# A turn through DRAM replaced by copies between partitions, and a last stage laid between late products

## The chip, the cores and the metric

The kernel runs on one core of a Trainium2 chip. The metric is the device time of one execution in microseconds. A core has a matrix engine (TensorE, PE in the profile, with its weight loads as PEld), a vector engine (VectorE, DVE), a scalar engine (ScalarE, ACT), GpSimd (POOL), and a sync engine (SP) that here only issues DMAs. ACT and POOL issue DMAs too. All DMAs run on the core's 16 DMA engines.

## The reference

The input is a sequence of 2048 rows of 512 channels, `x = A_u`. Two branches read it, and a gate per row mixes them:

```python
g = _sigmoid((x * gate_w).sum(-1, keepdims=True))
a = _A_ref(...)   # K[d,l] = sum_n Re(C exp(dt A l) dt B); y = irfft(rfft(u) * rfft(K)) + u * Dskip
b = _B_ref(...)   # gelu(x @ w1 + b1) @ w2 + b2, with an inner width of 1792
return g * a + (1 - g) * b
```

So `a` is a long convolution of every channel with a kernel K made from 128 complex exponentials, and `b` is a dense layer pair. All is float32.

## The kernel before

The program has two parts. `front` computes the gates, the dense branch `b` (already times 1 - g, written to `out`), the taps K and the first stage of the transforms of signal and taps. Every operation of it is a task with a due time; a planner (`Plan`) orders the tasks of each engine once, while the program is built, and the upper-case constants at the head of the file (`T_MLP`, `T_KG`, `D_KP` and so on) are the due times and offsets. The first stages' results go to DRAM: `tu_d` (signal) and `tk_d` (taps), 32 rows of 256 KB each. The last 18 products of the dense branch's second layer (each three matmuls, since a float32 factor is split into a high and a low part) are not planned; `front` hands them over as the list `late`.

`conv` is written out by hand, and each engine runs its instructions in the order of the program text. It works in 16 passes `s`, two transform rows n = 2s and 2s + 1 each:

- `signal(s)` and `taps(s)`: the second stage of the transforms on PE (tiles `p2u`, `p2k`, line 1157); ACT evicts `p2k`.
- `product(s)`: six DVE operations, the complex product.
- `inverse(s)`: the first stage back, on PE, into `pa` (line 1196).
- `turn(s)`: ACT copies `pa` to one of six buffers `sa`, and the data changes its layout: what lay on 128 partitions as (part, row) must lie, for the last stage, with transform rows on the partitions. Before, SP stores `sa` to DRAM (`t_d`, named `t4_d` in the code, line 1204), in groups of 8 rows; when a group is whole, POOL (ACT for the last row of all) fetches it as blocks of 8 or 4 rows onto every fourth partition of `t3` and `den` (line 1216). Some fetches wait in a list `held` until pass 9.
- `dense(k)`: fetches two tiles of the dense branch's result from `out` into `mos[k]`, in rooms that have come free (six by SP in passes 7 to 12, two by ACT behind the passes).

The late products run on PE by `rest(n)`, which takes n from the list, into four accumulators `acc` (lines 1241 to 1243): three before the last inverse, fifteen behind it. Then DVE adds each accumulator, times its gate, to its tile in `mos` (line 1293). The last stage has 8 blocks `m` (line 1301): each makes two result tiles `pb` by 8 matmuls as the profile counts them, and each of these reads a row block on all 128 partitions of `t3` or `den`, so every block needs all 32 turned rows. A tile is evicted by DVE with gate and dense part in one step (line 1313), or, for the six tiles in `ASIDE`, by ACT and then POOL. Blocks 0 to 6 go out by SP, 512 KB each (line 1317); the two tiles of block 7 by SP and ACT, 256 KB each (line 1315).

Rooms: `attic` (11 rows of 2 KB per partition), `loft` (8) and `den` (8) outlive the front. `places` deals them to the signal's rows `us[n]`: den's 8 first, then attic and loft, then 5 again from attic. 27 rows are fetched by `front` (`early`, line 479), the other 5 in the passes. The taps' rows `t2s` have eight buffers of their own (tag `tk`), and rows 16 to 23 use rooms of `t3`.

Of the kernel before, what the change touches and what calls it, by code (L numbers as in the profile page):

```python
# [9 lines left out]
F32 = mybir.dt.float32  # L10
# [3 lines left out]
ALU = mybir.AluOpType  # L14
# [3 lines left out]
P = 128  # L18
# [16 lines left out]
T_MLP = 408.145  # L35
K_0 = 32.114
T_KG = 351.806
U_0 = 29
U_GAP = 18
LAG = 14.812  # L40
TABLE = 27.405
D_KA = -32.407
D_KP = -80.929
D_S1 = 7.912
D_EV = -40.921
D_H = -80.673
# [3 lines left out]
D_SP = -0.52  # L50
MEM = (6, 2, 3)
N_LD, N_HL, N_ST = MEM
D_XS = -157.526
D_G = 1.227
N_WARM = 13
T_EARLY, T_LOFT, T_DEN = 353.026, 381.686, 484.328
Y_K, Y_U = 44.535, 26.725
W_MLP = (-0.0644, -0.031, 0.0179)
W_KG = (-0.0372, -0.0319, -0.0262)
W_U = (-0.0347, -0.139, -0.0186)  # L60
D_MAG = -0.783
D_ROT = 0.578
D_CON = 0.705
D_PHA = 0.305
D_PRE = -3.087
D_XL = 34
D_COE = -3.192
D_OUT = -3.305
D_LAST = -1.557
N_REST = 3  # L70
D_KA0 = 0
D_DT = 5
D_PRM = -277.043
D_D0 = -1024.07
D_WAVE0 = -343.734
D_COE0 = -66.219
D_SP1 = -461.8
D_G0 = 2
D_GW = 598.738
D_XS0 = 98.527  # L80
# [3 lines left out]
D_X0, D_B2, D_B2C, D_DM = -1313.069, -235.635, -950.754, -4.033  # L84
# [4 lines left out]
HERE, THERE = (7, 6, 0, 1, 2, 3), (4, 5)  # L89
N_DEN = 8  # L90
N_ROOM = N_ATTIC + N_LOFT
N_US = N_DEN + N_ROOM

GROUP = 8
# [19 lines left out]

def seat(n, c, kind):

    return 4 * (16 * kind + 2 * (n % 8) + c) + n // 8
# [11 lines left out]
def constants():  # L129
# [39 lines left out]
    g2 = np.zeros((32, 64, 32, 2))  # L169
    for n, k in enumerate(ko):  # L170
        er, ei = om(4 * np.outer(q - 31.5, k + 32 * k1) + (q - 31.5)[:, None])
        f2[n, 0], f2[n, 1] = er, -ei
        a = 2.0 * np.pi * (k + 32 * k1 + 0.25) / L
        g2[n, :, :, 0] = np.cos(np.outer(a, m))
        g2[n, :, :, 1] = np.sin(np.outer(a, m))
        g2[n, :, 0, 1] = 1 - 2 * (k1 % 2)
# [131 lines left out]
def gated_mix(  # L308
# [24 lines left out]
    t4_d = dr.tile([4, 2, GROUP, 2, 32, D], F32, name="t4_d")  # L333
# [11 lines left out]
    def places(attic, loft, den):  # L345

        rooms = [attic[:, k] for k in range(N_ATTIC)] + [loft[:, k * D : k * D + D] for k in range(N_LOFT)]
        return [den[:, k] for k in range(N_DEN)] + rooms + rooms[: 32 - N_US]

    def front(pool, psum, keep, attic, loft, den):  # L350
# [113 lines left out]
        def early():  # L464

            us = places(attic, loft, den)
            keys = [("ux", 0)] + [("st", k) for k in range(N_ST)]
            keys = [*keys, *(("ld", k) for k in range(N_LD)), "gwb"]
            yield 1e6
            for n in range(N_US):  # L470
                m = n - N_DEN
                if m < 0:
                    due, key = T_DEN + n, [("xc", n // 4)]
                elif m < N_ATTIC:
                    due, key = T_EARLY + 2.5 * m, [keys[m]]
                else:
                    due, key = T_LOFT + m, ["xt", "xv"] if m < N_ATTIC + 4 else ["tt"]
                move(
                    256, lambda n=n: nc.sync.dma_start(us[n], tu_d[k0_order()[n]]), due,
                    [("u_d", k) for k in range(64)], key,  # L480
                )
            yield None
# [636 lines left out]
    def conv(pool, ps, late, attic, loft, den):  # L1119
# [4 lines left out]
        us = places(attic, loft, den)  # L1124
# [73 lines left out]
        def turn(s):  # L1198

            for n in (2 * s, 2 * s + 1):  # L1200
                sa = sas[n % 6]
                nc.scalar.copy(sa, pas.pop(n))
                g, k = divmod(n, GROUP)
                nc.sync.dma_start(t4_d[g, :, k].rearrange("e c q d -> (c q) e d"), sa)
# [4 lines left out]
                for h in (0, 4, 8, 16, 24) if g == 3 else (0, 8, 16, 24):  # L1209
                    if h == 24 and g < 2:  # L1210
                        held.append((t3[g:P:4, 16:24], rows[:, 24:32]))
                        continue
                    on = nc.gpsimd if n < 31 else nc.scalar
                    e = h + (4 if g == 3 and h < 8 else 8)
                    to = t3[g:P:4, h - 8 : e - 8] if h > 7 else den[g:P:4, h:e]
                    on.dma_start(to, rows[:, h:e])

        accs, mos = {}, {}
        held = []

        def dense(k, on):

            q = HERE.index(k) if k in HERE else 6 + THERE.index(k)
            r = 5 + 2 * q if q < 7 else 0
# [5 lines left out]
            on.dma_start(mos[k], out[2 * k : 2 * k + 2].rearrange("s p d -> p s d"))  # L1230
# [27 lines left out]
        for s in range(16):  # L1258

            for n in range(2 * s + N_TK + (2 if s else 0), 2 * s + N_TK + 4):  # L1260
                if n < 24:
                    fetch(n if n < 16 else n + 8)
            if s == 0:
                for n in range(16, 24):
                    fetch(n)
# [11 lines left out]
            if s == 9:  # L1277
                for to, rows in held:
                    nc.gpsimd.dma_start(to, rows)
# [4 lines left out]
            if 7 <= s < 13:  # L1284
                dense(HERE[s - 7], nc.sync)
        for k in THERE:
            dense(k, nc.scalar)
        rest(18)

        for s in range(4):  # L1290
            m, i = 7 - s // 2, s % 2
            z, g = mos[m][:, i], gate[:, 1, 2 * m + i : 2 * m + i + 1]
            nc.vector.scalar_tensor_tensor(z, accs[s], g, z, ALU.mult, ALU.add)

        for m in range(8):
            tag = ("pu0", "pu1", "pu2", "pu3", "pa0", "pa1", "pk0", "pk1")
            pbs = [ps.tile([P, D], F32, tag=tag[(2 * m + i) % 8], name=f"pb{m}{i}", bufs=1) for i in range(2)]
            for i in range(2):
                for b in range(2):
                    j = 4 * m + 2 * i + b  # L1300
                    nc.tensor.matmul(  # L1301
                        pbs[i][64 * b : 64 * b + 64], g1t[:, min(j, 1)], t3[:, j - 8] if j > 7 else den[:, j],
# [13 lines left out]
            if m < 7:  # L1316
                nc.sync.dma_start(out[2 * m : 2 * m + 2].rearrange("s p d -> p s d"), mos[m])

# [4 lines left out]
    den = keep.tile([P, N_DEN, D], F32, name="den")  # L1323
# [76 lines left out]
```

## Time and profile before

| | us |
|---|---|
| timed runs: median of 3 (lowest, highest) | 520.37 (519.99, 521.77) |
| the profiled execution | 517.95 |
| its span, first to last instruction | 515.7 |
| PE busy | 501.5 |
| granted PE clock, mean | 0.995 |

The page gives the busy time of each engine, the span in 40 slices, the DMA queues, the chain of work that ended last (followed back from the last instruction to what released it), the costliest groups of instructions, and the DMA issues with their size and median time to landing. The other views used are busy times by windows, the chain in order of time, the instructions in order of time for one engine, and the instructions of one line or tile. A busy PE is not PE at its peak, since ends of matmuls are modelled; distances from start to start are safer. DMA moved 107.87 MB at a mean of 209 GB/s, 37.24 MB of it from 404 us to the end.

```
## 2 busy tenths in 40 slices
PE   7899999999999999999999999999999999999995
DVE  5999999999999996999999699979951188877543
ACT  5698846899685769995776997747733655555311
DMA  8965995522395331565753265967486998999978
```

### The profile page before, as it was taken

The numbers are of one execution on the slowest core, as the hardware profiler recorded it, in microseconds if no ns is written. First come the engines' busy times: TensorE is split into PE (matmuls) and PEld (weight loads), VectorE is DVE, ScalarE is ACT, GpSimd is POOL, SyncE is SP. The second block draws the span as 40 slices with busy tenths as digits, with TensorE's granted clock in tenths as the row PEclk, the third lists the DMA queues.
The fourth block names the chain that finished last, engine by engine and source line by source line (L and its number), as shares of the span: only waits on it lengthen the run. The fifth ranks groups of instructions, "written<-read, shape, count | busy, mean of one in ns | idle before, by whom it ended". The sixth has DMA issues, their size and how long they took to land.

```text
span 515.7 us, 12196 instructions
## 1 busy us (share of the span) xinstructions
PE 501.5 (97%) x4810; PEld 385.1 (75%) x4810; DVE 427.5 (83%) x792; ACT 349.6 (68%) x625; POOL 42.6 (8%) x82
## 2 busy tenths in 40 slices
PE   7899999999999999999999999999999999999995
PEld 6797898899888989898888977888989742222551
DVE  5999999999999996999999699979951188877543
ACT  5698846899685769995776997747733655555311
POOL 3000000000000000001001020101010100020113
PEclk9899999999999999999999999999999999999999
DMA  8965995522395331565753265967486998999978
GB/s 293 338 229 176 319 310 172 184 85 101 109 219 163 104 124 48 177 217 145 142 186 63 84 143 135 194 205 207 132 231 159 267 391 291 372 319 401 345 280 306
DMA packets 80008, 107.87 MB, mean 209 GB/s; under 512 B 39404, under 2 KB 40560, under 8 KB 79408
## 3 DMA queue, kind: packets, MB, share of 16 engines
q1 hardware_dynamic: 73904, 85.10, 50.9%
q0 software_dynamic: 5120, 18.59, 13.5%
q10 hardware_dynamic: 928, 3.41, 1.8%
q8 instruction: 38, 0.62, 0.5%
q14 instruction: 18, 0.15, 0.1%
HBM read 61.46 MB, written 45.62 MB: 208 GB/s over the span
## 4 chain that ended last, share of the span: by engine, by line
PE 79%; ACT 7%; DVE 7%; DMA 4%; issue 1%; SPq 1%; DVEq 0%; ACTq 0%
PE pk L724 10%; PE ph L946 8%; PE acc L994 8%; PE ph L948 8%; PE ph L947 8%; PE acc L996 7%; PE acc L995 7%; PE p2u L1157 6%; PE p2k L1157 5%; PE pa L1196 3%; PE pb L1301 3%; PE ph L436 3%; DMA tk<-tk_d 1%; DMA tu_d<-attic 1%; DMA sk<-in_w_dram 1%
## 5 line engine op out<-in xcount | busy, mean ns | idle before, releaser
L946 PE MATMUL ph<-xh,wh 128*128 128x256 f32 x448 | 128.1, 286 | 3.2 <-DVE hl L976 2.9
L948 PE MATMUL ph<-xh,wl 128*128 128x256 f32 x448 | 127.6, 285 | 1.4 <-DVE wl L826 1.4
L947 PE MATMUL ph<-xlo,wh 128*128 128x256 f32 x448 | 127.0, 284 | 0.0
L946 PEld LDWEIGHTS ph<-xh,wh 128*128 128x128 f32 x448 | 85.5, 191 | 10.7 <-issue 7.0
L948 PEld LDWEIGHTS ph<-xh,wl 128*128 128x128 f32 x448 | 85.6, 191 | 2.3 <-DVE wl L826 2.3
L947 PEld LDWEIGHTS ph<-xlo,wh 128*128 128x128 f32 x448 | 85.5, 191 | 2.0
L994 PE MATMUL acc<-wh,hh 128*128 128x512 f32 x206 | 83.1, 404 | 0.0
L996 PE MATMUL acc<-wh,hl 128*128 128x512 f32 x206 | 81.0, 393 | 0.9 <-DVE hl L976 0.8
L995 PE MATMUL acc<-wl,hh 128*128 128x512 f32 x206 | 81.1, 394 | 0.0
L963 ACT ACTIVATE ph<-ph,b1t 128x256 f32<-128x256 f32 x112 | 50.5, 451 | 39.2 <-PE ph L948 37.4
L724 PE MATMUL pk<-y,den 128*32 128x64 f32 x2048 | 61.4, 290 | 0.0
L724 PEld LDWEIGHTS pk<-y,den 128*32 128x32 f32 x2048 | 57.2, 136 | 3.5 <-issue 1.8
L976 DVE TENSOR_TENSOR hl<-ph,hh 128x512 fp32r<-128x512 f32 (+1 forms) x62 | 38.1, 616 | 19.2 <-ACT hh L966 19.1
L994 PEld LDWEIGHTS acc<-wh,hh 128*128 128x128 f32 x206 | 39.0, 189 | 16.2 <-issue 8.6
L687 DVE TENSOR_TENSOR y<-y,ea 128x64 f32<-128x64 f32 (+4 forms) x80 | 45.2, 564 | 4.1 <-ACT y L677 3.3
L996 PEld LDWEIGHTS acc<-wh,hl 128*128 128x128 f32 x206 | 38.8, 189 | 10.5 <-DVE hl L976 1.8
L995 PEld LDWEIGHTS acc<-wl,hh 128*128 128x128 f32 x206 | 38.8, 189 | 6.5
L966 ACT CAST hh<-ph 128x512 fp32r<-128x512 f32 (+1 forms) x62 | 33.0, 532 | 13.6 <-PE acc L995 12.0
L530 DVE TENSOR_TENSOR loft<-den,zz 128x256 f32<-128x256 f32 (+2 forms) x48 | 37.2, 775 | 0.6
L531 DVE TENSOR_TENSOR loft<-den,zz 128x256 f32<-128x256 f32 (+2 forms) x48 | 37.1, 773 | 0.0
L699 DVE TENSOR_TENSOR y<-y,loft 128x2048 f32<-128x2048 f32 x16 | 36.5, 2283 | 0.0
L1165 ACT COPY k<-p2k 128x512 f32<-128x512 f32 x32 | 18.7, 585 | 25.1 <-issue 13.1
(194 smaller groups left out, 873.8 us busy)
## 6 DMA issues: line engine op xcount, KB each, us to landing
tu_d<-attic SPq DMA_DIRECT2D x64, 128.0 KB, 3.6
tk_d<-sk SPq DMA_DIRECT2D x32, 256.0 KB, 4.9
t_d<-sa SPq DMA_DIRECT2D x32, 256.0 KB, 5.2
tk<-tk_d SPq DMA_DIRECT2D x24, 256.0 KB, 5.1
t<-t_d POOLq DMA_DIRECT2D x9, 512.0 KB, 7.3
attic<-in_xt_dram SPq DMA_DIRECT2D x16, 256.0 KB, 4.3
attic<-in_xs_dram SPq DMA_DIRECT2D x16, 256.0 KB, 4.6
xh_d<-xh SPq DMA_DIRECT2D x8, 512.0 KB, 3.6
```

Of the source, the lines that this page charges most:

```text
L530: vec(2 * m, lambda: vv.tensor_mul(t, a, br), due, [ka, *kb], [kt])
L687: nc.vector.tensor_mul(both(n, 64 - 3 * n, n), both(0, 64 - n, n), an)
L724: nc.tensor.matmul(pks[q][32 * j : 32 * j + 32, :, gg], x[:, r, :, ch], y[:, r, :, ch], start=(r == 0), stop=(r == 1), skip_group_check=True,)
L946: nc.tensor.matmul(p, h, xh[xk][:, d], start=(d == 0), stop=False)
L947: nc.tensor.matmul(p, h, xlo[xk][:, d], start=False, stop=False)
L948: nc.tensor.matmul(p, lo, xh[xk][:, d], start=False, stop=(d == 3))
L963: nc.scalar.activation(phs[q][:, n], phs[q][:, n], AF.Gelu_apprx_tanh, bias=b1t[:, f : f + 1])
L976: nc.vector.tensor_sub(lo, phs[q][:, 0:nf], hi.bitcast(F32))
L994: nc.tensor.matmul(a, h, wh[1][w], start=start, stop=False)
L995: nc.tensor.matmul(a, h, wl[1][w], start=False, stop=False)
L996: nc.tensor.matmul(a, l, wh[1][w], start=False, stop=(j == 3))
L1157: nc.tensor.matmul(out[64 * i : 64 * i + 64], w, x, start=True, stop=True)
```

## The change

Three things change in `conv`, and the plan's constants with them.

1. The turn: `t4_d` and the fetches are gone. POOL copies each `sa` straight from its 128 partitions to four partitions of `t3` (64 KB in each), whose tile now has all 32 rows. `seats(n)` says which: four partitions with a distance of 4; the next n goes to the other half of the partitions (64 n%2), then to 16 further, then to 32 further. The constants `g1` and `g2` are laid out for the new order.
2. The late products: three ahead of the last inverse as before, then nine, then two behind each of the blocks 0, 1 and 2 of the last stage. The four DVE steps of the accumulators follow block 3. The PSUM banks of the blocks are dealt accordingly.
3. The rooms: `den` holds the eight buffers of the taps' rows. The signal has 19 rooms (attic, loft); 19 rows are fetched by `front`, 13 in the passes. All eight dense fetches are SP's, in passes 7 to 14.

```diff
-T_MLP = 408.145
+T_MLP = 408.543
-T_KG = 351.806
-U_0 = 29
+T_KG = 350.709
+U_0 = 28
-D_KP = -80.929
-D_S1 = 7.912
+D_KP = -71.841
+D_S1 = -20.915
-D_LAST = -1.557
-N_REST = 3
+D_LAST = -10.576
+N_REST, N_FIRST = 3, 9
...
+PAIRS = ((7, 13), (6, 15), (0, 17), (1, 0), (2, 2), (3, 4), (4, 6), (5, 8))
+N_US = N_ATTIC + N_LOFT
...
+def seats(n):
+
+    b = 64 * (n % 2) + 16 * (n // 2 % 2) + 32 * (n // 4 % 2) + n // 8
+    return slice(b, b + 13, 4)
+
+
 def seat(n, c, kind):
 
-    return 4 * (16 * kind + 2 * (n % 8) + c) + n // 8
+    return seats(n).start + 4 * (2 * c + kind)
...
         def fetch(n):
-            if 16 <= n < 24:
-                t2s[n] = t3[:, n]
-            else:
-                t2s[n] = pool.tile([P, D], F32, tag="tk", name=f"tk{n}", bufs=N_TK)
+            t2s[n] = den[:, n % N_TK]
             nc.sync.dma_start(t2s[n], tk_d[ko[n]])
...
                 nc.scalar.copy(sa, pas.pop(n))
-                g, k = divmod(n, GROUP)
-                nc.sync.dma_start(t4_d[g, :, k].rearrange("e c q d -> (c q) e d"), sa)
-                if k < GROUP - 1:
-                    continue
-                rows = t4_d[g].rearrange("e k c q d -> (e k c) q d")
...
-                    on.dma_start(to, rows[:, h:e])
+                nc.gpsimd.dma_start(t3[seats(n)], sa)
...
-                t3 = pool.tile([P, 24, D], F32, name="t3", bufs=1)
+                t3 = pool.tile([P, 32, D], F32, name="t3", bufs=1)
...
-            for n in range(2 * s + N_ROOM, min(2 * s + N_ROOM + 2, 32)) if s > 3 else ():
+            for n in range(2 * s + N_US, min(2 * s + N_US + 2, 32)):
                 nc.sync.dma_start(us[n], tu_d[ko[n]])
...
             if s == 15:
                 rest(N_REST)
             inverse(s)
             turn(s)
-            if 7 <= s < 13:
-                dense(HERE[s - 7], nc.sync)
-        for k in THERE:
-            dense(k, nc.scalar)
-        rest(18)
-
-        for s in range(4):
-            m, i = 7 - s // 2, s % 2
-            z, g = mos[m][:, i], gate[:, 1, 2 * m + i : 2 * m + i + 1]
-            nc.vector.scalar_tensor_tensor(z, accs[s], g, z, ALU.mult, ALU.add)
+            if 7 <= s < 15:
+                dense(*PAIRS[s - 7])
+        rest(N_FIRST)
 
         for m in range(8):
-            tag = ("pu0", "pu1", "pu2", "pu3", "pa0", "pa1", "pk0", "pk1")
...
+            tag = ("pu0", "pu1") if m in (0, 2, 4) else ("pa0", "pa1") if m < 6 else ("pu2", "pu3") if m == 6 else ("pk0", "pk1")
...
             if m < 7:
                 nc.sync.dma_start(out[2 * m : 2 * m + 2].rearrange("s p d -> p s d"), mos[m])
+            rest(2 if m < 3 else 18)
+            if m == 3:
+                for s in (2, 3, 0, 1):
+                    z, g = mos[7 - s // 2][:, s % 2], gate[:, 1, 14 - s // 2 * 2 + s % 2 : 15 - s // 2 * 2 + s % 2]
+                    nc.vector.scalar_tensor_tensor(z, accs[s], g, z, ALU.mult, ALU.add)
```

Some thirty other constants of the plan move by a little (`U_0`, `T_EARLY`, the `D_` offsets); the tasks that they order are the same, but for the eight fetches that leave the front.

More of the change, by code (lines that the diff above doesn't have):

```diff
@@ L343, in gated_mix, with places @@
     c1t = cp.tile([P, 64], F32, name="c1t")
-    def places(attic, loft, den):
+    def places(attic, loft):
         rooms = [attic[:, k] for k in range(N_ATTIC)] + [loft[:, k * D : k * D + D] for k in range(N_LOFT)]
-        return [den[:, k] for k in range(N_DEN)] + rooms + rooms[: 32 - N_US]
+        return rooms + rooms[: 32 - N_US]
     def front(pool, psum, keep, attic, loft, den):
@@ L464, in early @@
         def early():
-            us = places(attic, loft, den)
+            us = places(attic, loft)
             keys = [("ux", 0)] + [("st", k) for k in range(N_ST)]
@@ L1123, in conv @@
         zs = [pool.tile([P, D], F32, name=f"z{k}", bufs=1) for k in range(2)]
-        us = places(attic, loft, den)
+        us = places(attic, loft)
         ko = k0_order()
@@ L1202, in turn, with dense @@
                 nc.scalar.copy(sa, pas.pop(n))
-                g, k = divmod(n, GROUP)
-                nc.sync.dma_start(t4_d[g, :, k].rearrange("e c q d -> (c q) e d"), sa)
-                if k < GROUP - 1:
-                    continue
-                rows = t4_d[g].rearrange("e k c q d -> (e k c) q d")
[L1209 to L1216, printed above, removed]
+                nc.gpsimd.dma_start(t3[seats(n)], sa)
         accs, mos = {}, {}
[L1219 to L1224, printed above, removed]
+        def dense(k, r):
             if r < N_ATTIC:
```

96 lines of the change are left out of this document (40 added, 56 removed).

## The prediction

> **What bounds the kernel now.** I read the page first (how busy each engine is, the chain that ended last), then the busy time by windows, then the chain near the end, then the timelines of ACT, SP and DVE there, and the DMA issues.
>
> ```profile
> span 515.7 us, 12196 instructions
> PE 501.5 (97%) x4810; PEld 385.1 (75%) x4810; DVE 427.5 (83%) x792; ACT 349.6 (68%) x625; POOL 42.6 (8%) x82
> ```
> ```profile
> 0.00:50.00 50.00, 43.87 (x269) 38.73 (x270) 42.29 (x108) 38.05 (x75) 5.20 (x18) 0.97 0.74 262
> 50.00:100.00 50.00, 49.89 (x550) 42.36 (x550) 49.60 (x101) 36.69 (x64) 0.25 (x2) 1.00 0.71 240
> 300.00:395.00 95.00, 93.05 (x1141) 80.43 (x1140) 77.62 (x138) 63.05 (x103) 10.91 (x18) 1.00 0.69 178
> 405.00:415.00 10.00, 9.89 (x56) 6.75 (x56) 4.26 (x8) 5.53 (x12) 0.00 (x0) 1.00 1.06 314
> 415.00:482.00 67.00, 67.00 (x353) 19.03 (x349) 54.23 (x90) 37.72 (x71) 6.31 (x12) 1.00 0.97 350
> 482.00:496.00 14.00, 14.00 (x68) 10.32 (x66) 4.44 (x8) 2.15 (x4) 0.00 (x0) 1.00 0.83 286
> 496.00:510.00 14.00, 13.82 (x64) 4.37 (x63) 7.63 (x11) 4.12 (x6) 7.46 (x6) 1.00 0.94 359
> ```
> The columns of a window are its stretch and length, then PE, PEld, DVE, ACT and POOL busy, the granted clock, the share of the DMA engines and GB/s. The first number behind the length is what counts: from 415 to 496 PE does not stop, so nothing there but PE's own work sets the time. PE is idle for 515.7 - 501.5 = 14.2 us in all: 6.13 in the first 50 us, 0.11 in the next 50, 1.95 between 300 and 395, 0.11 where the convolution begins, and nearly all the rest behind the last product. DMA is very full in the 16 passes (0.97), but PE never waits for it.
>
> ```profile
> 474.72 1.87 PE p2u L1157 x8
> ...
> 479.33 1.87 PE p2u L1157 x8
> 481.19 1.02 PE pa L1196 x8
> 482.21 0.43 PE acc L1241
> 482.64 0.23 PE acc L1242
> ...
> 484.25 0.23 PE acc L1243
> 484.48 1.02 PE pa L1196 x8
> 485.50 0.43 PE acc L1241
> ...
> 495.71 0.23 PE acc L1243
> 495.94 13.91 PE pb L1301 x64
> ...
> 509.87 0.75 DVE attic L1313
> ```
> This is the chain, in order of time. A pass lasts 479.33 - 474.72 = 4.61 us. Then come three late products (nine matmuls) ahead of the last inverse, the other fifteen from 485.50 to 495.94, the last stage's 64 matmuls in one piece of 13.91 us, one eviction on DVE, and the output DMAs, until 515.7. The chain has no wait in it from 409.67 on.
>
> **The change, part by part.** *The turn.* Removed: 32 stores of 256 KB to t_d by SP, and the fetches of 512 or 256 KB from it by POOL and ACT. Added: 32 copies of 256 KB from sa to four partitions of t3, on POOL's queue. 8.4 MB less go through the DMA engines. That is worth nothing by itself: PE hides the old transfers, as its unbroken 67 us show. Two copies' issue per pass have room on POOL, which is busy 6.31 us in those 67. SP's fetches no longer stand behind the stores that wait for ACT. The copies have two deadlines. The first: sa has six buffers, so copy n must land before ACT writes sa again three passes, 3 x 4.61 = 13.8 us, later; past that, ACT stops, and with it the evictions of p2k that PE needs. The second is the last copy, for every block of the last stage reads all the rows of t3.
>
> ```profile
> 485.60 1.07 ACT L1202 COPY sa<-pa 128x512 f32<-128x512 f32 x2 [2.20 <-issue]
> 402.40 1.72 POOL L1027 DMA_DIRECT2D out_dram<-io  x2 [21.12 <-ACT io L1016]
> L1204 SPq DMA_DIRECT2D t_d<-sa x6: 518/538/1431, 480.0 to 486.8; - x6
> 491.49 1.16 ACTq L1216 DMA_DIRECT2D den<-t_d  x2
> out_dram<-io POOLq DMA_DIRECT2D x14, 256.0 KB, 5.6
> t<-t_d POOLq DMA_DIRECT2D x9, 512.0 KB, 7.3
> den<-t_d ACTq DMA_DIRECT2D x2, 256.0 KB, 3.0
> ```
> ACT writes the last two sa by 486.67, the first at some 486.2. A POOL issue of 128 rows of 2 KB takes 1.72 / 2 = 0.86 us, so the last copy's issue starts near 487.1. How long such a copy to four partitions takes, the trace does not show. From below: 3.0 us, the quickest 256 KB here, lands it at 490.1. From above: 7.3 us, POOL's 512 KB under load, at 494.4. The nearest row is the same sa on its way to DRAM: issued at 486.8, used at 491.49, so at most 4.7 us; POOL's own 256 KB takes 5.6, but accumulates. I take 4.9, between them, and nearer the first: 492.0.
>
> [...]
>
> PE comes to the last stage after rest(9): 27 matmuls from 485.50 at (495.94 - 485.50 - 0.20) / 45 = 0.228, and 0.20 for the first (below), end at 491.85. **Wait: 492.0 - 491.85, about 0.2 us** (bounds 0 and 494.4 - 491.85 = 2.6).
>
> *Blocks between the late products.* The same 45 and 64 matmuls run, but PE goes between the kinds more often. Before, it goes from acc to pb once behind the last inverse; now after rest(9), and after each of three rest(2): three more round trips. Into acc: the first costs 0.43 where the next cost 0.23, so 0.20. Into pb:
>
> ```profile
> 496.35 0.14 PEld L1301 LDWEIGHTS pb<-den,g1t 128*64 128x64 f32 x2 [0.29 <-issue]
> 496.78 0.14 PEld L1301 LDWEIGHTS pb<-den,g1t 128*64 128x64 f32 x2 [0.29 <-issue]
> ```
> Two matmuls per 0.43 make 32 x 0.43 = 13.76 of 64; the piece took 13.91, so 0.15. Three round trips: **3 x 0.35 = 1.05 us**, all on PE, with nothing beside it. If the step into pb were free, as the one from acc to pa is (1.02 both times), it would be 0.6.
>
> *DVE's four gate steps of the accumulators* move from among the late products to behind block 3. A block is 8 matmuls, 1.72 us, so PE needs 4 x 1.72 = 6.88 us from the end of block 3 to its last product.
>
> ```profile
> 481.09 0.68 DVE L1180 TENSOR_TENSOR v<-p2u,k 128x512 f32<-128x512 f32 x1
> 481.69 0.68 DVE L1181 TENSOR_TENSOR z<-p2u,k 128x512 f32<-128x512 f32 x1
> ```
> DVE has ten steps from there on (block 3's own, the four, and those of tiles 9, 10, 12, 14 and 15). Nine at 0.75 end to end are 6.75, so the tenth starts in time; as the rows show steps overlapping a little, there is some air. Cost 0; without that air, a tenth or two.
>
> *The output.* Block 0 ends near 493.9 instead of 497.8, block 1 two microseconds sooner, blocks 3 to 7 about one later. What ends the span is the last megabyte:
>
> ```profile
> 508.50 2.08 SPq L1317 DMA_DIRECT2D out_dram<-attic  x2
> 510.68 0.42 SPq L1315 DMA_DIRECT2D out_dram<-attic  x1
> 505.00:507.00 2.00, 2.00 (x12) 0.65 (x10) 1.23 (x2) 0.56 (x1) 0.91 (x1) 1.00 1.00 383
> 511.50:512.50 1.00, 0.00 (x0) 0.00 (x0) 0.00 (x0) 0.00 (x0) 0.00 (x0) 1.00 1.02 387
> ```
> Block 6's 512 KB leave at 510.2 and the two last 256 KB at 510.7. 1.05 MB at 387 GB/s is 2.7 us, about the time from 511 to the last byte near 514. This depends on the last blocks alone, which run as before: 0. If an older backlog still stood in front, up to 0.6 us would go.
>
> *The rooms.* den holds the taps' eight buffers and no early signal rows; 19 rows are loaded early, not 27, and 13 in the passes.
>
> ```profile
> 400.49 1.23 SPq L479 DMA_DIRECT2D den<-tu_d  x2
> 402.74 6.89 DMA tk<-tk_d
> 409.67 1.93 PE p2k L1157 x6
> ```
> Two of the eight loads stood in SP's queue ahead of the first taps, which land as PE runs dry (0.11 idle). They go, so the taps come about 1.2 us sooner: worth 0.1 at most. The 13 later fetches come several passes ahead of use. Cost 0.
>
> *The constants of the plan.* They reorder the first 400 us. PE's work there is the same, so only its idle time can move: the 1.95 us between 300 and 395 might go, or as much again be drawn. I take 0.
>
> Sum: 0.2 + 1.05 + 0 = **+1.25 us**. The profiled execution took 517.95 us, its span 515.7; so about 517.0 of span. The three timed runs lie higher, 520.37 in the median, and I add the sum to that: 521.6.
>
> **The rivals.** *Faster, by idle time.* The new plan takes out the 1.95 us, the output's backlog goes (0.6), the steps between kinds cost 0.6, and the start's 6.13 us give a few tenths: 520.37 + 0.6 - 1.95 - 0.6 - 0.4 = 518.0; a good part of it, not all, is likelier, about 518.8. For it: the waits between 300 and 395 are short ones on DVE, which an order can avoid. Against: nothing says that the new constants do.
>
> *The last copy lands late.* At 7.3 us PE waits 2.6 instead of 0.2: 520.37 + 1.05 + 2.6 = 524.0. Against: the only heavy loads left then are long done, as the output has not begun. A new plan with idle time of its own would give about the same.
>
> *Slower: the copies don't run side by side.* 383 GB/s at a full share is 24 GB/s per engine. If one copy has only four engines, 96 GB/s, it takes 2.7 us. If the next one waits for it, because it falls to the same engines or ports, two need 5.5 us per pass of 4.61. It decides from 2.3 us per copy on. Then ACT stands at sa and PE behind it, 16 x 0.86 = 14 us: 534, or more with the loads on the same engines. The trace cannot exclude it. [...]
>
> *It does not do what it says*: the copies land early, PE is still bound by its own work, and the price of the steps between kinds is all that is seen, 521.4. That is the forecast without its wait.
>
> **How the numbers follow.** Forecast with its neighbours (wait 0 to 0.5, front within 1 us): 0.48. Faster by idle time: 0.30. Late landing or a worse plan: 0.15. Copies in a row: 0.07. A measurement here can tell about 0.3%, 1.56 us, from no change: 518.81 and 521.93 are the marks. Of the forecast's 0.48, some 0.32 lies below 521.93 and 0.16 above. Of the 0.30, 0.22 goes below 518.81, the rest stays within. Of the 0.15, 0.03 stays within. So faster 0.22, same 0.43, slower 0.16 + 0.12 + 0.07 = 0.35. Range: 518.0, the faster case in full, to 524.6, the late landing with 0.6 from the plan; outside are the copies in a row and a little at either end.
>
> **What would show it.** Right: passes of 4.61 us with no PE idle time; in the chain, acc and pb in turn four times, each first acc 0.43; PE's work from the last inverse to the last pb 25.4 us (24.35 now) and a wait below 0.5 ahead of the first pb. Wrong: passes longer than 4.7 with ACT's copy to sa waiting on a DMA; a wait of over 1 us ahead of the first pb; PE's idle time up to 395 changed by over 1 us; or a span that ends less than 5.3 us after the last pb (5.85 now).

## The result, and the profile after

| | before | after |
|---|---|---|
| timed runs: median of 4 (lowest, highest), us | 520.27 (519.99, 521.77) | 550.01 (548.52, 551.42) |
| ratio of the times, 95% interval | | 1.0565 (1.053 to 1.06) |
| profiled execution, us | 517.95 | 551.42 |
| its span, us | 515.7 | 549.5 |
| granted PE clock, mean | 0.995 | 0.979 |

The kernel became 5.6% slower; the forecast was 521.6, its range 518.0 to 524.6. From the page of the changed kernel, the first lines and two of the DMA issues:

```profile
span 549.5 us, 12173 instructions
PE 513.9 (94%) x4810; PEld 384.2 (70%) x4810; DVE 426.5 (78%) x792; ACT 349.4 (64%) x625; POOL 58.1 (11%) x102
den<-tk_d SPq DMA_DIRECT2D x32, 256.0 KB, 9.4
t<-sa POOLq DMA_DIRECT2D x32, 256.0 KB, 13.2
```

PE is idle for 549.5 - 513.9 = 35.6 us, where it was 14.2. The new copies land 13.2 us after their issue, and the taps' fetches, which the change gives another room and a later place in the passes, 9.4 us after theirs (before 5.1, in either room). The windows of the changed kernel say where (stretch and length, then PE, PEld, DVE, ACT and POOL busy, granted clock, DMA share, GB/s):

```profile
0.00:50.00 50.00, 42.82 (x269) 37.48 (x270) 42.32 (x108) 38.16 (x75) 5.27 (x18) 1.00 0.74 262
300.00:395.00 95.00, 93.85 (x1143) 81.22 (x1142) 77.66 (x138) 62.75 (x102) 10.95 (x18) 1.00 0.65 163
415.00:482.00 67.00, 54.78 (x244) 14.40 (x240) 37.96 (x63) 26.94 (x51) 12.90 (x20) 0.90 0.91 223
482.00:496.00 14.00, 13.70 (x68) 4.01 (x70) 9.84 (x17) 7.15 (x14) 3.26 (x5) 1.00 1.00 217
496.00:510.00 14.00, 12.20 (x56) 3.88 (x52) 7.37 (x12) 3.92 (x7) 4.03 (x6) 1.00 1.01 240
...
443.50:448.00 4.50, 4.49 (x8) 1.18 (x8) 0.00 (x0) 0.59 (x1) 0.00 (x0) 0.50 0.95 251
```

The front is nearly as before. In the passes, PE is busy 54.78 of 67 us. The last two numbers of a row matter most: the DMA engines are as busy as before (0.91 to 1.01, before 0.97), but move 217 to 240 GB/s, where they moved 350. Engine time per byte has gone up by half. The experiments below show that DMA, which was hidden behind PE, became the bound.

The waits of the changed kernel (engine, what, releaser: us in total, times, longest), PE's first, then one of ACT's:

```profile
PE p2k L1152 <- DMA den<-tk_d: 12.5, 4, 5.0
PE pb L1266 <- DMA t<-sa: 6.3, 1, 6.3
...
PE p2k L1152 <- issue: 1.7, 1, 1.7
...
ACT sa L1197 <- DMA t<-sa: 6.9, 3, 3.6
```

And its timelines, SP's first, then PE's, ACT's and POOL's (start, us, what, the idle time before it and who ended that):

```profile
417.24 0.80 SPq L1133 DMA_DIRECT2D den<-tk_d  x2
...
423.37 3.12 SPq L1244 DMA_DIRECT2D attic<-tu_d  x2
426.53 5.38 SPq L1133 DMA_DIRECT2D den<-tk_d  x2
432.01 7.36 SPq L1244 DMA_DIRECT2D attic<-tu_d  x2
439.47 4.80 SPq L1133 DMA_DIRECT2D den<-tk_d  x2
...
443.51 2.11 PE L1152 MATMUL p2k<-den,cc 128*64 128x512 f32 x3 [4.99 <-DMA den<-tk_d]
...
448.11 1.09 PE L1191 MATMUL pa<-v,cc 64*64 64x512 f32 x8
...
473.50 2.42 PE L1152 MATMUL p2k<-den,cc 128*64 128x512 f32 x3 [5.02 <-DMA den<-tk_d]
...
478.40 1.26 PE L1191 MATMUL pa<-v,cc 64*64 64x512 f32 x8
...
507.79 2.19 PE L1191 MATMUL pa<-v,cc 64*64 64x512 f32 x8
...
512.45 1.08 ACT L1197 COPY sa<-pa 128x512 f32<-128x512 f32 x2 [3.59 <-DMA t<-sa]
...
513.33 1.34 POOL L1198 DMA_DIRECT2D t<-sa  x2 [3.51 <-ACT sa L1197]
...
522.64 3.68 PE L1266 MATMUL pb<-t,g1t 128*64 128x512 f32 x8 [6.31 <-DMA t<-sa]
```

Three things are to be seen. SP issues two loads in 0.80 us until 418; from 423.37 to 444.27 the issue of eight takes 20.66 us, and no idle time is shown between them: the issue itself stands. (The view of SP's waits puts 5.9 us of this to PE's `p2u`. But the rooms of the two signal rows issued from 432.01 on had been read by 424.7, so this is no wait for a room.) PE stands for the taps that come so late (4.99 us, later 5.02). And what follows such a wait is slow: eight matmuls of `p2k` from 443.51 to 448.11, in 4.60 us instead of 1.72, since the granted clock is 0.50 there (the last window row). After the second wait they take 478.40 - 473.50 = 4.90.

From the view of single lines and tiles of the changed kernel, the issues of the taps' fetches (min/median/max in ns) and the landing of the copies:

```profile
L1133 SPq DMA_DIRECT2D den<-tk_d x32: 319/474/3951, 401.3 to 486.3; - x32
...
DMA to landing us min/median/max: 6.8/13.2/17.5
```

The longest issue of a taps' row took 3.95 us, the longest of a signal row 4.72.

The end of the chain of the changed kernel:

```profile
514.00 8.19 DMA t<-sa
522.19 0.46 issue
522.64 3.68 PE pb L1266 x8
526.33 0.57 PE acc L1220
528.06 1.87 PE pb L1266 x8
529.93 0.43 PE acc L1220
531.51 1.87 PE pb L1266 x8
533.38 0.43 PE acc L1220
534.98 8.76 PE pb L1266 x40
543.76 0.75 DVE loft L1278
```

The 33.8 us of span split as follows. The first `p2u` of the chain starts at 410.35 instead of 411.60: -1.25. From there to the end of the last inverse it takes 507.79 + 2.19 - 410.35 = 99.63 instead of 485.50 - 411.60 = 73.90: +25.73. From there to the end of the last `pb` it takes 534.98 + 8.76 - 509.98 = 33.76 instead of 24.35: +9.41, of which 6.31 is the wait for the last copy, 3.68 - 1.87 = 1.81 the half clock behind it, and the rest, 1.29, the three round trips. The tail is 5.76 instead of 5.85.

The 25.73 can be split by PE's timeline, from one `pa` to the next. The five passes in which PE waits ahead of `p2k` are longer than 4.61 by 7.94, 2.85, 8.27, 1.58 and 2.82 us, two others by 0.74 and 0.38. The last inverse takes 2.19 us instead of 1.02, because its second half waits until ACT, held up at `sa`, has evicted the `pa` before. That makes 25.75.

### The profile page after: what moved, and what is told of

The parts are those of the page before. It is cut to its first block, busy times and chain, and to the rows that moved or that the text cites. A ratio compares the mean times of both kernels' runs of the same rounds, so it can differ in the third digit from the quotient of the medians.

```text
span 549.5 us, 12173 instructions
## 1 busy us (share of the span) xinstructions
PE 513.9 (94%) x4810; PEld 384.2 (70%) x4810; DVE 426.5 (78%) x792; ACT 349.4 (64%) x625; POOL 58.1 (11%) x102
## 4 chain that ended last, share of the span: by engine, by line
PE 68%; issue 14%; DVE 6%; ACT 4%; POOL 3%; DMA 2%; SPq 0%; POOLq 0%; DVEq 0%
PE pk L722 10%; PE ph L944 9%; PE acc L992 8%; PE ph L946 8%; PE ph L945 8%; PE acc L994 8%; PE acc L993 8%; POOL t L1198 3%; PE pb L1266 3%; PE ph L437 2%; DMA t<-sa 1%; DVE wl L824 1%; PE p2k L1152 1%; DMA sk<-in_w_dram 1%; PE p2u L1152 1%
## 5 line engine op out<-in xcount | busy, mean ns | idle before, releaser
L1174 DVE TENSOR_TENSOR v<-p2u,k 128x512 f32<-128x512 f32 x16 | 11.1, 691 | 39.9 <-ACT sa L1197 23.3
L528 DVE TENSOR_TENSOR loft<-den,zz 128x256 f32<-128x256 f32 (+2 forms) x48 | 37.2, 774 | 0.6
L1152 PE MATMUL p2k<-den,cc 128*64 128x512 f32 x64 | 24.2, 660 | 14.3 <-DMA den<-tk_d 12.5
## 6 DMA issues: line engine op xcount, KB each, us to landing
t<-sa POOLq DMA_DIRECT2D x32, 256.0 KB, 13.2
```

Source lines behind the costliest of these rows:

```text
L528: vec(2 * m, lambda: vv.tensor_mul(t, a, br), due, [ka, *kb], [kt])
L1152: nc.tensor.matmul(out[64 * i : 64 * i + 64], w, x, start=True, stop=True)
```

## Experiments

Each kernel is the changed one with the edit shown, unless another is named. "Before" is the kernel before on the same chip. An interval stands where runs were repeated.

### Whose part is it: old_turn, late_first, act_copies

`old_turn`: the turn of before through DRAM, with all late products ahead of the last stage; what is left of the change is rooms, fetches, dense order and constants.

```diff
-                nc.gpsimd.dma_start(t3[seats(n)], sa)
+                nc.sync.dma_start(t4_d[g, :, k].rearrange("e c q d -> (c q) e d"), sa)
...
+                    on.dma_start(t3[g:P:4, h:e], rows[:, h:e])
```

> The kernel after with the turn of before (store to DRAM by SP, fetches in groups of eight rows) and all late products ahead of the last stage; rooms, plan constants and dense fetches are those of after. Theory A (the copies to four partitions cost the passes their 25.7 us): passes of 4.61 us again, no PE wait for the taps, 518 to 521 us. Theory B (eight tap buffers and 13 signal fetches in SP's queue make the taps late, whatever the turn): PE still waits over 10 us for den<-tk_d, 535 us or more.

528.69 us, ratio 1.0159 (1.0093 to 1.0225): between what the two theories gave. Most of the loss goes with the copies, but some 8 us stay when the old turn runs in the new rooms. The waits and one window of `old_turn`:

```profile
PE p2k L1149 <- DMA den<-tk_d: 4.1, 1, 4.1
```
```profile
445.00:475.00 30.00, 24.68 (x119) 7.10 (x117) 20.51 (x34) 12.86 (x24) 2.09 (x4) 0.98 1.02 376
```

The share is full here too, but at 376 GB/s. It is again the taps that come late.

`late_first`: all 15 late products ahead of the last stage (and DVE's four steps behind them).

```diff
-        rest(N_FIRST)
+        rest(18)
```

> The kernel after with all 15 late products ahead of the last stage (the copies kept). If the 6.3 us wait for the last copy and the three extra steps between kinds are what the interleaving costs, six products (4.1 us) fill the wait and 1.05 us of steps go: 5 us less than after, about 544 to 545. If the wait moves along with it, within 1.5 us of 550.

545.17 us, near the 544 to 545 of the first expectation. But six more products, 18 matmuls or 4.1 us, stand ahead of the first `pb`, and its wait fell only from 6.3 us to 4.0; and in this single run the waits ahead of `p2k` came to 11.3 us instead of 15.0, with the same passes. So the blocks' place is at most a small part of the 30 us.

`act_copies`: ACT issues the copies.

```diff
-                nc.gpsimd.dma_start(t3[seats(n)], sa)
+                nc.scalar.dma_start(t3[seats(n)], sa)
```

> The kernel after with the 32 copies issued by ACT instead of GpSimd. [...] If the partitions' ports limit the copies and the engines do not, it stays at 545 to 555.

580.82 us, above the 545 to 555 that ports as the limit were to give. From the waits of `act_copies`:

```profile
PE p2k L1152 <- ACT f L1141: 38.5, 7, 11.3
```

ACT stands at its copies and cannot evict, for 38.5 us of PE's time. The DMA engines have a share of only 0.64 from 415 to 482 us, at 186 GB/s. What keeps the share down is not shown: no view shows single engines, and an issuer that also has to evict would lose time with slow copies in any case.

### Bytes, queue, seats or shape: plain_copies, no_copies, no_dense, swap_seats

`plain_copies`: the same 256 KB per copy, by the same queue, from 128 partitions to 128 partitions of one row block; the data is not turned.

```diff
-                nc.gpsimd.dma_start(t3[seats(n)], sa)
+                nc.gpsimd.dma_start(t3[:, n], sa)
```

> The kernel after with each copy of 256 KB going from sa to one row block of t3 over all 128 partitions (the rows are not turned, so the last stage reads other data); issuer, bytes, waits and order are those of after. Theory A (the shape with four partitions, four engines per copy, costs the time): the passes run at 4.61 us, no wait ahead of the last stage, 518 to 521 us. Theory D (the bytes of the copies beside the fetches of the new rooms are too much): 540 us or more.

519.48 us, ratio 0.9983 (0.9955 to 1.001). A window of `plain_copies`, and its taps' fetches (duration of an issue, min/median/max in ns; then of the landing in us):

```profile
415.00:482.00 67.00, 67.00 (x353) 18.77 (x350) 54.29 (x90) 37.58 (x71) 14.98 (x29) 1.00 0.91 322
```
```profile
L1133 SPq DMA_DIRECT2D den<-tk_d x32: 319/428/895, 401.8 to 459.1; - x32
DMA to landing us min/median/max: 3.9/6.5/9.1
```

PE does not stop. The DMA share is the 0.91 of the changed kernel, but at 322 GB/s instead of 223, and the longest issue of a taps' row is 0.9 us. With everything else of the change in place, the shape of the copies alone makes the 30 us.

`no_copies`: GpSimd sets the rows of `t3` to zero instead of copying, so the convolution's part of the output is left out.

```diff
-                nc.gpsimd.dma_start(t3[seats(n)], sa)
+                nc.gpsimd.memset(t3[:, n], 0.0)
```

> The kernel after with a GpSimd memset of the row block of t3 in place of each copy (the turn is left out). Both theories expect passes of 4.61 us and 517 to 520 us; if PE still waits for the taps, the new rooms and SP's order alone make them late (theory B), 525 us or more.

517.67 us, no wait for taps in the passes. A turn that cost nothing at all would give this, about the time of before.

The DMA view from 415 to 482 us splits the share by queue (packets, MB, share of 16 engines): `q1` are the loads that SP issues, `q0` GpSimd's copies. Both of the changed kernel, then the copies of `plain_copies`, then the loads of `no_copies`:

```profile
q1 hardware_dynamic: 5674, 10.15, 54.2%
q0 software_dynamic: 4885, 4.75, 37.1%
...
q0 software_dynamic: 2240, 7.34, 28.6%
...
q1 hardware_dynamic: 7865, 14.28, 65.4%
```

So 256 KB (0.262 MB) to four partitions held 0.371 x 67 x 16 / (4.75 / 0.262) = 22 us of engine time, and the same bytes to 128 partitions 11. An estimate from these rows: in a pass of 4.61 us sixteen engines have 74 us. The loads of a pass take 48 in the mean (0.654 x 67 x 16, over 67 / 4.61 passes). With two copies to 128 partitions that is 70, which fits; with two to four partitions it is 92, which needs a pass of 5.8 us, or 18 us more in 16 passes. Of the measured 25.73, the half clock takes 6.1 and the last inverse 1.2, and 18.4 are left. The estimate is rough: alone, in `probe_beside`, such a copy held 18 us (0.142 x 8 x 16), which would give 11, and shares above 1 (1.08 in `early_fetch`) say that the times of packets overlap a little.

`no_dense`: GpSimd sets the dense tiles to zero instead of SP fetching them, so most of the dense branch's part is left out.

```diff
-            nc.sync.dma_start(mos[k], out[2 * k : 2 * k + 2].rearrange("s p d -> p s d"))
+            nc.gpsimd.memset(mos[k], 0.0)
```

> The kernel after with a GpSimd memset in place of each fetch of the dense branch's tiles in passes 7 to 14 (4.2 MB less; the dense part up to the late products is left out). Theory A with fetches held up by the copies: the wait in pass 5, ahead of the dense fetches, stays, and part of those behind it, 530 to 542 us. If the dense fetches are what collides, only a microsecond or two above before, 519 to 524.

535.87 us, as the first expectation had it: eight fetches of 512 KB less give back 14 us. PE still waits 4.2 us for taps and 3.9 ahead of the first `pb`.

`swap_seats`: the next n goes 16 partitions further first, then to the other half.

```diff
-    b = 64 * (n % 2) + 16 * (n // 2 % 2) + 32 * (n // 4 % 2) + n // 8
+    b = 16 * (n % 2) + 64 * (n // 2 % 2) + 32 * (n // 4 % 2) + n // 8
```

> The kernel after with the two inner steps of the seats exchanged: neighbours 16 partitions apart, then 64 (the rows are turned as before). If it matters which group of engines meets which ports, the time moves by more than 5 us from 550, either way; if the number of engines per copy alone matters, 546 to 554.

549.87 us, against 550.01: which of these seats the next copy gets made no difference here.

### How many partitions: copies_8, copies_16

Each copy goes to 8 or 16 partitions, with half or a quarter of the bytes in each; the rows then stand in other places than the last stage expects.

```diff
-                nc.gpsimd.dma_start(t3[seats(n)], sa)
+                b, r = 64 * (n % 2) + n // 2 % 4 + 32 * (n // 8 % 2), n // 16
+                nc.gpsimd.dma_start(t3[b : b + 29 : 4, 16 * r : 16 * r + 16], sa)
```

> The kernel after with each copy going to 8 partitions and half of the row blocks (rows not turned, so the last stage reads other data); neighbours lie in different halves of the partitions. Theory A (few engines per copy): alone such a copy took 4.0 us against 6.3 to 8.0, so most of the loss goes, 521 to 530 us. If only the write into few partitions of the last copy and not its engines matters, the passes keep their waits for the taps, 535 us or more.

> The same with 16 partitions and a quarter of the row blocks. Theory A: all 16 engines share each copy (2.9 us alone), the time is that of plain copies, 518 to 521 us. If the source, 128 partitions read in long runs, is what hurts, it stays above 530.

527.04 and 521.82 us. With 550.0 for 4 partitions and 519.5 for 128, the loss falls by three quarters at the first doubling. `copies_16` lies a little above its 518 to 521, with 1.5 us of waits for taps left: over 16 partitions a copy still held 15 us of engine time (a share of 0.343 for its 32 copies, from 410 to 500 us).

### The copy by itself: probe_alone, probe_spread

Single transfers of 256 KB behind the output, each group after the one before has landed. The first of each probe still ran beside the output's last stores.

```diff
+        fence()
+        nc.gpsimd.dma_start(t3[0:13:4], sas[0])
+        fence()
+        nc.gpsimd.dma_start(t3[0:4], sas[0])
...
+        nc.gpsimd.dma_start(t3[0:29:4, 0:16], sas[0])
...
+        nc.gpsimd.dma_start(t3[0:13:4], tu_d[0])
```

> The kernel after, and behind its output a row of transfers of 256 KB one after the other on an idle machine; the output is unchanged. [...] Theory C (ports): neighbouring partitions take much longer than partitions 4 apart, four copies at once no longer than one. [...]

> The kernel after, and behind its output single transfers of 256 KB by GpSimd, each alone: four times the same copy from sa to four partitions, then to 8, 16 and 32 partitions 4 apart, from DRAM to four partitions, from SBUF to DRAM as 4, 16 and 128 rows, from DRAM to four neighbouring partitions, and 8 KB to four partitions. Four engines alone as the cause: 8 us for 4 partitions, half of the transfer part for 8, a quarter for 16, and SBUF to DRAM with four rows the same 8. If reading 32 partitions of SBUF per engine is what slows it (from DRAM it took 5.1), SBUF to DRAM with four rows takes 7 or more as well; if writing, 5 to 6. If it matters which engines meet which ports, the four equal copies differ by over 1 us.

| 256 KB, by GpSimd | us to landing |
|---|---|
| sa to 4 partitions 4 apart, alone | 6.6, 6.3, 7.2 |
| the same, beside the output's last stores | 8.0, 8.0 |
| sa to 8, 16, 32 partitions | 4.0, 2.9, 2.3 |
| sa to 128 partitions | 2.4 |
| sa to 4 neighbours | 11.9 |
| DRAM to 4 partitions 4 apart | 5.1, 4.9 |
| DRAM to 4 neighbours | 11.2 |
| two sa copies, four sa copies, at once | 7.2 to 8.1, 8.9 to 9.6 |

So the forecast's 4.9 us for the copy was too short by 1.4 to 2.3 with nothing beside it; the same copy from DRAM took just that. Copies from `sa` to different partitions do run side by side: four at once, issued within 2 us, each landed within 9.6 us of its issue, where four in a row at 6.3 would need 25. Theory C is not all of it: neighbours took much longer, 11.9 us, as it has it, but four copies at once took longer than one, 8.9 to 9.6 us against 6.3 to 7.2. The equal copies alone differ by 0.9 us, less than the 1 us that was to show a matter of which engines meet which ports. Some groups of the probes ran into one another, and the stores in rows had a contiguous target, so nothing is read from these.

### Engines or ports: probe_beside, copies_to_dram

`copies_to_dram`: the copies write four rows of 64 KB in DRAM that nobody reads; GpSimd sets `t3` to zero, and the convolution's part is left out.

```diff
-                nc.gpsimd.dma_start(t3[seats(n)], sa)
+                nc.gpsimd.dma_start(t4_d[n, :, 0:32], sa)
+                if n % 4 == 3:
+                    nc.gpsimd.memset(t3[:, n - 3 : n + 1], 0.0)
```

> The changed kernel with each copy sent to four rows of 64 KB in DRAM that nothing reads, instead of to four partitions; the rows that the last stage reads are set to zero by GpSimd, so the convolution's share of the output is left out. Same issuer, bytes, and number of rows; no partition is written by the copies. Engine share: the four rows still put each copy on four engines, so the passes are as after's, with waits for den<-tk_d of some 8 to 13 us in all, and the time is 535 to 546, which is after's 550 less its wait of 6.3 ahead of the first pb and less the clock that this wait cost. Ports: the passes are unbroken and the time is 516 to 521, as without the copies (517.7).

534.62 us, just below the 535 to 546 of engine share and far from the 516 to 521 of ports. Waits of `copies_to_dram`, and the issues of its taps' fetches:

```profile
PE p2k L1153 <- issue: 6.4, 2, 4.5
PE p2k L1153 <- DMA den<-tk_d: 4.4, 3, 3.0
```
```profile
L1134 SPq DMA_DIRECT2D den<-tk_d x32: 319/542/3940, 402.1 to 480.2; - x32
```

SP's issues stand as in the changed kernel, up to 3.9 us, though no copy writes to a partition, and a copy held 20 us of engine time (a share of 0.358 for 6.89 MB, from 410 to 500 us). Four rows per copy are enough for it. Whether the rest of the difference to the changed kernel belongs to the partitions that are written is not settled: that one also waits for its last copy.

`probe_beside` has single copies with four rows, and loads beside copies of several kinds.

```diff
+        nc.gpsimd.dma_start(tk_d[0:4, 0:32], tu_d[8])
...
+        for n in range(4):
+            nc.gpsimd.dma_start(t3[seats(n)], sas[n])
+            nc.sync.dma_start(den[:, n], tu_d[n])
```

> The changed kernel, and behind its output single transfers, each group after the one before has landed: 256 KB as four rows from sa to DRAM and from DRAM to DRAM, from DRAM and from sa to four partitions, then four loads of 256 KB to 128 partitions alone, and the same four loads beside four copies of one kind each: sa to four partitions, DRAM to four partitions, DRAM to DRAM in four rows, sa to 128 partitions, sa to DRAM in four rows. The output is as before. Alone the loads landed in 2.6 to 4.0 us, and copies beside loads in 10 to 11.3. If the copies harm the loads because each keeps four of the sixteen engines busy for long (engine share), all kinds with four rows do it: the last load lands in 6 to 9 us beside each of them, and in some 5 beside the copies to 128 partitions. If the harm lies with the few partitions that are written (their ports), the last load lands in 4 to 5.5 beside the four rows to DRAM, and in 6 to 9 only beside the two kinds that write four partitions. A copy to four rows in DRAM alone takes 6 to 8 us by the first theory, under 3.5 by the second.

Four loads alone landed in 2.8 to 4.1 us, beside four copies from `sa` to four partitions in 6.2 to 13.6. The groups of the other kinds ran into one another (eight copies together, loads in 17.9 to 23.3), so nothing can be said of one kind against another. Alone, 256 KB from DRAM took 5.0 us to four rows in DRAM and 5.1 to four partitions, between the two theories: from DRAM it made no difference here whether four rows of DRAM or four partitions 4 apart were written. From `sa` to four rows in DRAM it took 8.9 us, but beside the output's last stores. From `probe_beside`, a window in the single copy from `sa` to four partitions; then the DMA view's packets, for that copy and for the one from DRAM:

```profile
572.00:576.00 4.00, 0.00 (x0) 0.00 (x0) 2.01 (x3) 0.00 (x0) 0.00 (x0) 0.50 0.23 57
```
```profile
DMA packets 272, 0.26 MB, mean 33 GB/s; under 512 B 208, under 2 KB 208, under 8 KB 272
...
DMA packets 32, 0.26 MB, mean 44 GB/s; under 512 B 28, under 2 KB 28, under 8 KB 28
```

A single copy keeps a mean share of 0.23 of 16 engines busy, as much as about four, and moves 57 GB/s. From `sa` it runs as 64 packets of 4 KB (272 less 208 small ones), from DRAM as four of 64 KB (32 less 28): that goes with the 6.7 us of the one and the 5.1 of the other here, and is no proof of the cause. The small packets are a rival to the count of engines: with 64 of 4 KB taken off, a copy from `sa` to 4 partitions brings 208 of them, to 8 partitions 80, to 16 or 128 partitions 16 (GpSimd's queue has 272 packets for the single copy and, from 410 to 500 us, 4624 for 8.43 MB in `copies_8`, 2560 for 8.39 MB in both `copies_16` and `plain_copies`). They are not all of it, since `copies_16`, with 16 per copy, still held more engine time than the copies to 128 partitions; how much of the loss is theirs was not tested.

### The plan: before_plan

The kernel before with the plan's constants of after.

```diff
-T_MLP = 408.145
+T_MLP = 408.543
...
-D_LAST = -1.557
+D_LAST = -10.576
```

> The kernel before with the plan constants of after (due times of the eight fetches into den kept). In after the second stage began 1.25 us sooner than in before. If the constants did that, 1 to 1.5 us less than before, about 518.7, hardly to be told from no change; if the smaller number of early fetches did it, no change.

518.44 us, ratio 0.9988 (0.9964 to 1.0012): no change that can be measured.

### Lead or rate: early_fetch, old_early

With eight buffers, a pair of taps' rows can be fetched as soon as the pair four before it has been read. The changed kernel fetches it one pass later than that. Before fetched one pass sooner, and it had rooms of `t3` for eight more rows of taps, so its last fetch of taps starts at 447.4 us, that of the changed kernel at 486.3. Both kernels here (`early_fetch` from the changed one, `old_early` from `old_turn`) take the one pass back.

```diff
-            for n in range(2 * s + N_TK, min(2 * s + N_TK + 2, 32)):
+            for n in range(2 * s + N_TK + (2 if s else 0), min(2 * s + N_TK + 4, 32)):
                 fetch(n)
```

> The changed kernel with each pair of taps' rows fetched one pass sooner, as the kernel before does with its eight buffers (in pass s rows 2s+10 and 2s+11 instead of 2s+8 and 2s+9); nothing else differs. A fetch then has about three passes, 13.8 us, instead of two, 9.2, until PE needs it. Short lead: landings of 9.4 us in the median with up to 4 us of issue ahead of them fit into 13.8, so the 14.2 us that PE waits for den<-tk_d fall below 5, and the time is 530 to 541, with the wait ahead of the first pb still there. Rate: SP's queue drains too slowly beside the copies however early a fetch stands in it, so the first wait moves by a pass and the sum stays: 545 to 551.

> The kernel of old_turn (the changed kernel with the turn of before through DRAM and all late products ahead of the last stage) with the same earlier fetches. Short lead: the 5.3 us that old_turn's PE waits for den<-tk_d go, as the landing there is 6.4 us in the median, and the time falls from 528.7 to 519 to 524. Rate: the DMA engines are full from 445 to 482 in old_turn, so the same bytes come no sooner: 526 to 531.

548.8 us for `early_fetch`, ratio 1.055 (1.0491 to 1.0609); 523.2 for `old_early`, ratio 1.0064 (1.0036 to 1.0091). Waits and a window of `early_fetch`:

```profile
PE p2k L1152 <- DMA den<-tk_d: 11.5, 9, 3.9
PE pb L1266 <- DMA t<-sa: 4.4, 1, 4.4
```
```profile
445.00:475.00 30.00, 23.64 (x95) 6.00 (x96) 13.99 (x23) 9.76 (x19) 4.40 (x7) 0.94 1.08 249
```

The same stretch of `old_early`:

```profile
445.00:475.00 30.00, 29.91 (x158) 8.22 (x152) 22.95 (x38) 17.09 (x33) 2.10 (x4) 1.00 1.03 393
```

This parts the two losses. Beside the old turn the lead was too short: with the pass back, the waits for taps are gone, and some 5.5 us with them; a wait of 2.3 us ahead of the first `pb` is left. (Behind the like wait of `old_turn`, 2.2 us, the 64 matmuls of the last stage took 15.67 us instead of 13.91.) Beside the new copies the same pass gives nothing measurable, the waits only spread (9 instead of 4, 11.5 us instead of 12.5): the loads' rate is too low, at a full share and 249 GB/s, where the old turn reaches 393. No kernel of the study is faster than before by more than the runs scatter.

## Why the prediction was wrong

**The step that failed first** is the one that put the bytes at nothing: "8.4 MB less go through the DMA engines. That is worth nothing by itself: PE hides the old transfers". It counted bytes; what was scarce is the engines' time. They had a share of 0.97 in the passes, a row that the prediction quoted. A copy to four partitions held 22 us of engine time where the same bytes to 128 partitions held 11, so the share stays full at two thirds of the rate (223 against 350 GB/s; 322 with the same bytes in another shape). The loads pay: 9.4 us to land, SP's issue of eight in 20.66 us, PE's 14.2 us of waits ahead of `p2k` (12.5 put to the taps, 1.7 to nothing that the view shows), and the half clock behind the two longest, 4.60 + 4.90 - 2 x 1.72 = 6.1. The waits, the clock and the last inverse make 21.5 of the 25.73; the rest lies around the shorter waits of the same passes. That the shape of the copies makes the loss is shown; what in the shape costs the engine time, few engines or many small packets, stays open.

**The copy's own term** was mis-sized: 4.9 us against 6.3 to 7.2 alone and 13.2 among loads. The upper end, 7.3, came from a transfer to 32 partitions, and 256 KB to 32 partitions landed in 2.3 us alone; it was no bound for one to four. (Nor was 3.0 the quickest 256 KB: `out_dram<-io` by SP has 2.7 in the median.) The wait ahead of the first `pb` was 6.31 us instead of 0.2. The late products ahead of it were there, but the last two copies were issued only at 513.33, behind ACT's wait of 3.59 us for the buffers of `sa`: the deadline of 13.8 us, which the prediction set, was missed by copies that take 13.2 in the median and up to 17.5.

**The rooms** were put at nothing, with an eye on the signal's fetches alone. The fetches of the taps, in lines of the change that are not among those shown, came a pass or more closer to their use. `old_turn` against `old_early` shows what one pass costs beside the old turn: 528.7 against 523.2 us. In the change itself no cost of it is shown: `early_fetch` gains nothing that can be measured, and `plain_copies`, with the same rooms and fetches, runs at 519.48 us without a wait for taps. So the reasoning had a gap here, but the 30 us do not come from it.

**The rival that came nearest**, copies in a row on four engines, had a chance of 0.07 and a time of "534 or more". That a copy has four engines, and so 96 GB/s and 2.7 us, was the author's assumption, and no run shows it: a copy alone held a share of 0.23 of 16 engines, as much as about four, but moved 57 GB/s and landed in 6.3 to 7.2 us (from DRAM in 4.9 to 5.1). Its "or more", for the loads, is what happened, though no view shows on which engines, and its price was too small, because it let ACT's stand at `sa` (three waits, 6.9 us) be the whole loss. Its form was wrong too: copies run side by side (two at once landed in 7.2 to 8.1 us, one alone in 6.3 to 7.2). The 580.8 us with ACT as issuer do not decide it, since ACT's own stand, 38.5 us of PE's waits, is mixed into them.

**What held.** The three round trips: each later first `acc` took 0.43 us, each later block 1.87 = 8 x 0.215 + 0.15. DVE's four steps cost nothing: behind the last block stands one DVE step, as before, and the tail is 5.76 us. The front: the passes start 1.25 us sooner, where 0 was put down; PE's idle time moved by +1.05 in the first 50 us and by -0.80 between 300 and 395, and `before_plan` shows no effect of the constants that can be measured. What made the 1.25 is open; the granted clock from 20 to 30 us was 0.83 in the profile of before and 1.00 in that of the changed kernel. In sum these terms came to 1.29 - 1.25 - 0.09 = -0.05 us, where 1.05 was put down; that the sum is so close is partly luck, since the first two cancel.

## What to carry to other kernels

Where DMA has a share near 1 and hides behind PE, price a new transfer in engine time, not in bytes: by the share that one such transfer holds and for how long, and then ask what the loads beside it have left. Look for slowed issues of the loading engine (up to 4.72 us here, 0.98 beside the plain copies), and for GB/s falling at an unchanged share (322 to 223 at 0.91); both led to the cause sooner than the wait itself. The copy that gathers 128 partitions into four cost less over more partitions at once (527 and 522 us for 8 and 16, single runs, still not faster than before).

## What was not expected of the hardware

- The issue of a load on SP's queue took 0.32 us at least and 0.47 in the median, but up to 3.95 for a taps' row and 4.72 for a signal row beside the copies to four partitions (0.9 and 0.98 beside copies to 128).
- 256 KB from SBUF to 4, 8, 16 and 32 partitions alone landed in 6.3 to 7.2, 4.0, 2.9 and 2.3 us; to four neighbouring partitions in 11.9.
- Among the loads of the passes, 256 KB to four partitions held 22 us of DMA engine time, to 128 partitions 11.
- The same copy to four partitions from DRAM took 4.9 to 5.1 us, less than from SBUF.
- Behind idle stretches of 5.0 to 6.3 us PE's granted clock was 0.50 for some microseconds, which cost 1.81 us at the first block of the last stage beside the 6.31 of the wait itself. Behind waits of 1.74 and 1.76 us it was 1.00 (461.5 to 466 and 499.7 to 501.7 us). In `old_turn`, behind a wait of 2.2 us, the last stage's 64 matmuls took 15.67 us instead of 13.91.
